# Cumulative sums of logs as two float32r numbers, and closings of rows moved a step, in an attention and mixture-of-experts kernel

## The chip, the cores and the metric

The program runs on one core of one Trainium2 chip. Its time is the device time of one execution in microseconds (us). Times of the kernel before: a median of 416.69 us over 10 runs (415.75 to 418.52). The profile shown is that of one execution of 416.84 us.

Engines are named as in the profile: PE is TensorE (matmuls), PEld its weight loads, DVE VectorE, ACT ScalarE, POOL GpSimd, SP SyncE, which here only issues transfers.

## The reference

Attention comes first: 4 batches, 8 heads, 768 tokens, head size 48. For every batch and head a 48 x 48 state is carried over the tokens, with one decay per key channel:

```python
f = 1.0 / (1.0 + np.exp(-f_logit))
for t in range(S):
    state = f[:, :, t, :, None] * state + np.einsum('bhd,bhe->bhde', k[:, :, t], v[:, :, t])
    y[:, :, t] = np.einsum('bhd,bhde->bhe', q[:, :, t], state)
```

The heads of a token are joined to rows x (3072 x 384). A gate picks one of 4 groups for each row, a second gate one of the group's 4 experts; each gate's weight is that of a softmax. The result of a row is

```python
out[tok_idx] = (g_w * e_w)[:, None] * (np.maximum(x @ w1[g, e], 0.0) @ w2[g, e])   # w1 384 x 1024, w2 1024 x 384
```

## The kernel before

**Units and stages.** The 768 tokens are cut into 6 chunks of 128. A chunk with two of the four batches (s = 0 or 1) is a unit; there are 12, numbered 0 to 11 (NU = 12). With cs the running sum over a chunk's tokens of log(1 + exp(-f_logit)), that is of minus log f, the decay from the start of the chunk is exp(-cs). So a unit needs eq = exp(-cs) for q, kh = exp(cs) for k, masked products of the two for the tokens inside the chunk, and the state for what came before. Each unit goes through stages, each a Python generator that is advanced one piece at a time:

- l (load, L568 to L575): transfers of k, q, f and v, issued on SP's queue. `l` of unit j also issues f of unit j+1. The tiles of f rotate over 3 buffers.
- c (bounded, L581): DVE clamps f at -44 (128 x 768 numbers).
- g (gated): ACT makes exp (L591) and log (L594) in place, `nl`. Then for each of the unit's two batches a float32 matmul with the triangle of ones `tri` sums over tokens (L600, `cs`), and ACT makes eq and kh from it (L601, L602). For s = 0 and s = 1 the last row of eq goes to the tile `ends` by a transfer that POOL issues (L607).
- m (multiplied): DVE multiplies q by eq (L620) and k by kh (L623).
- t (turned): PE transposes both (L634), ACT copies them out (L635, Tq and Tk).
- b (decayed, odd units): PE transposes `ends` (L643, gt), ACT copies it (L644, decays).
- s (scored): PE makes the products `ap` of keys and queries (L659), DVE masks them with `tri` into `am` (L662).
- n (stated): PE makes k v (L676, ds); DVE adds it to the old state (L682, sp) and multiplies by the decays (L683).
- w (weighed): PE makes y from the state (L697) and from `am` (L701); ACT copies it to xT (L704).
- d (done): PE multiplies xT by the gates' weights (L717), ACT copies (L719), PE transposes (L722), DVE reduces to logits (L723, `lgs`).
- x (listed): PE transposes xT to rows (L742); ACT copies them. Rows of units 0 to 7 wait in SBUF and are sent later by SP (`send_kept`, letter o); later units' rows are sent by POOL or ACT.

After the second unit of a chunk, `route` (L178 to L256, letter r, a few pieces a step) picks group and expert on DVE, counts rows per expert with small bf16 matmuls (L203, L205, `rk`), gives each row a place (L211 to L224), and adds to a table of rows by place with bf16 matmuls (L251, `tb`, from `ln` L226 and `val` L233). Between val and the table DVE finishes the weight of each row (L236 to L244: sm, ew, ws, meta), POOL puts the token's number beside it (L245) and sends both to the row in DRAM (L246).

**Chunk 3** (CLOSE = NC - 3) ends with a ranking: after its counts DVE ranks the experts (L271 to L289, `who`), and SP loads the weights of those with most rows (L381). Its places lead to `rows_e` (L318), and after L305 POOL fetches the first rows of two experts (L393, `xg`), which waits for the transfers that write rows and weights of chunks 0 to 3. The expert passes follow: PE transposes xg (L429), multiplies by w1 (L439, `hp`) and w2 (L460, L475, `yo`).

**Order.** Orders are written out by hand and kept as written on PE, DVE, ACT and SP (L85, `manual_schedule`); POOL's order is the framework's. `BEGIN` lists the stages of steps 0 to 2, `EVEN` and `ODD` those of a step i, `ORDERS` the exceptions (NU-3 is step 9, NU-2 step 10, and so on). A token such as `g+1` is the next piece of stage g of unit i+1. A step in the middle takes 10.7 us. In step i PE turns and scores unit i, sums the logs of unit i+1 (after the transposes and before the scores), while c and g prepare the logs of unit i+2. So DVE clamps unit i+2 behind `am`, ACT makes its exp and log behind that. In an odd step b and the update of the state of unit i-1 stand ahead of the sums; in even steps of 4, 6, 8 and 10 tb and the closing of the rows' weights stand after them. PSUM has 8 banks, shared by all products.

Before the loop of steps (L839) SP sends two small "blank" transfers (L841, L842) for row 0 of the rows in DRAM.

## Time and profile before

| | |
|---|---|
| profiled execution | 416.84 us: span 415.0 and 1.84 around it |
| median of 10 runs | 416.69 us |
| attention until the first hp | 137.37 us from the span's start |
| busy: PE, DVE, ACT, POOL | 98%, 64%, 38%, 20% |
| L600 cs, mean of 48 records | 507 ns (a float32 matmul leaves two records) |
| cs of an even step (72.94 us) to the next matmul | 1.29 us |
| am of step 3, step 9, step 10 start | 43.85, 109.30, 120.11 us |

A line of a timeline gives start, duration, engine, line, operation, output and inputs, shapes, and in brackets how long the engine had been idle and what released it. A line of a group gives, after the count, busy time in us, mean ns of one, and idle time before them with its releasers. "L600" is line 600 of the kernel before. In the rows of slices each digit is a tenth of the span's fortieth; PEclk is the granted clock in tenths of full speed, 9 being 90% or more.

### The profile page before, as it was taken

What the parts mean: (1) busy time and instruction counts of PE and PEld (TensorE: products, weight loads), DVE (VectorE), ACT (ScalarE), POOL (GpSimd) and SP (SyncE); (2) the same over time, 40 slices, a digit from 0 to 9 for tenths busy, and PEclk for the clock granted to TensorE, in tenths of its full rate; (3) what the DMA queues carried; (4) which work ended last, traced back from release to release, by engine and by line L of the source; (5) the groups of instructions that cost most, each with busy time, mean ns of one, the idle gap of its engine ahead of it and who ended that gap; (6) DMA issues with size and microseconds to landing.
All of it is one profiled execution on the core that took longest, in us unless ns stands there. A gap on an engine that the chain in (4) does not pass through costs nothing.

```text
span 415.0 us, 10066 instructions
## 1 busy us (share of the span) xinstructions
PE 405.7 (98%) x4047; PEld 374.7 (90%) x4047; DVE 266.9 (64%) x778; ACT 157.1 (38%) x353; POOL 83.2 (20%) x127
## 2 busy tenths in 40 slices
PE   8999999999998999999999999999999999999995
PEld 3888988888777978989999999999999999999992
DVE  5666887878898731640799767485595595594230
ACT  6777766666555311211223122222231231231220
POOL 4000010101012147001041221311321320120230
PEclk9999999999999999999999999999999999999999
DMA  9999997877999649985729467586595695585010
GB/s 173 213 199 213 187 177 149 152 140 154 285 331 392 201 168 339 390 285 185 276 82 336 134 246 263 163 321 187 189 349 153 235 337 186 204 319 162 28 47 24
DMA packets 132145, 88.98 MB, mean 214 GB/s; under 512 B 102582, under 2 KB 122748, under 8 KB 132090
## 3 DMA queue, kind: packets, MB, share of 16 engines
q1 hardware_dynamic: 125666, 75.50, 62.2%
q0 software_dynamic: 5792, 11.92, 9.6%
q10 hardware_dynamic: 632, 0.83, 0.6%
q8 instruction: 34, 0.56, 0.6%
q14 instruction: 21, 0.17, 0.1%
HBM read 78.71 MB, written 9.83 MB: 213 GB/s over the span
## 4 chain that ended last, share of the span: by engine, by line
PE 48%; issue 30%; DMA 9%; POOL 6%; DVE 4%; ACT 1%; POOLq 1%
PE hp L439 12%; PE yo L475 7%; DMA out_dram<-yt,xg 6%; PE ap L659 5%; PE y L701 5%; PE yo L460 4%; POOL out_dram L450 4%; PE cs L600 4%; POOL xg L393 2%; PE x_ps L742 2%; PE ds L676 2%; PE tr_k L634 2%; PE tr_q L634 2%; PE y L697 2%; DMA xg<-x_dram,rows_e 2%
## 5 line engine op out<-in xcount | busy, mean ns | idle before, releaser
L439 PE MATMUL hp<-xe,w 128*128 128x128 f32 (+14 forms) x864 | 138.6, 320 | 0.0
L439 PEld LDWEIGHTS hp<-xe,w 128*128 128x128 f32 x864 | 135.8, 190 | 0.8
L475 PE MATMUL yo<-h,w 128*128 128x230 f32 (+13 forms) x672 | 115.8, 333 | 0.0
L422 DVE STREAM_TRANSPOSE yr<-yT 32x192 f32<-32x192 f32 (+1 forms) x208 | 70.5, 339 | 70.4 <-ACT yT L476 67.8
L475 PEld LDWEIGHTS yo<-h,w 128*128 128x128 f32 x672 | 113.7, 190 | 0.2
L415 DVE STREAM_TRANSPOSE xe<-xg 32x192 f32<-32x192 f32 (+1 forms) x208 | 69.7, 335 | 8.6 <-PE hp L439 5.6
L440 ACT ACTIVATE h<-hp 128x256 f32<-128x256 f32 (+14 forms) x72 | 34.4, 478 | 103.6 <-PE hp L439 103.6
L450 POOL DMA_INDIRECT out_dram<-yt,xg x32 | 34.4, 1075 | 150.0 <-ACT yt L447 144.4
L476 ACT COPY yT<-yo 128x230 f32<-128x230 f32 (+13 forms) x42 | 13.4, 325 | 80.5 <-PE yo L475 80.5
L393 POOL DMA_INDIRECT xg<-x_dram,rows_p x30 | 29.6, 987 | 51.9 <-DMA out_dram<-yt,xg 28.2
L662 DVE TENSOR_TENSOR am<-ap,tri 128x512 f32<-128x512 f32 x48 | 29.8, 681 | 11.2 <-PE ap L659 11.2
L701 PE MATMUL y<-am,v 128*64 128x128 f32 x384 | 24.7, 276 | 0.6 <-issue 0.4
L701 PEld LDWEIGHTS y<-am,v 128*64 128x64 f32 x384 | 21.1, 137 | 4.0 <-issue 2.5
L659 PE MATMUL ap<-Tq,Tk 48*64 48x128 f32 x768 | 23.8, 273 | 0.0
L659 PEld LDWEIGHTS ap<-Tq,Tk 48*64 48x64 f32 x768 | 20.8, 133 | 1.6 <-issue 1.1
L460 PE MATMUL yo<-w,h 128*128 128x384 f32 x64 | 21.3, 486 | 0.0
L600 PE MATMUL cs<-ld_f,tri 128*128 128x384 f32 x48 | 18.6, 507 | 0.1
L460 PEld LDWEIGHTS yo<-w,h 128*128 128x128 f32 x64 | 11.9, 190 | 7.4
L607 POOL DMA_DIRECT2D ends<-eq x10 | 5.4, 541 | 55.5 <-ACT eq L601 55.5
L447 ACT ACTIVATE yt<-yr,xg 128x384 f32<-128x384 f32 (+13 forms) x26 | 14.4, 604 | 5.4 <-DVE yr L422 5.4
L704 ACT COPY xT<-y 128x512 f32<-128x512 f32 x24 | 13.5, 581 | 5.2 <-PE y L701 5.1
L634 PE MATMUL tr_q<-ident,qh 128*128 128x128 f32 x96 | 14.5, 273 | 0.5 <-issue 0.4
(173 smaller groups left out, 369.4 us busy)
## 6 DMA issues: line engine op xcount, KB each, us to landing
w<-in_moe_w_dram SPq DMA_DIRECT2D x34, 1536.0 KB, 10.5
qh<-in_q_dram SPq DMA_DIRECT2D x12, 384.0 KB, 4.9
ld_k<-in_k_dram SPq DMA_DIRECT2D x12, 384.0 KB, 6.0
v<-in_v_dram SPq DMA_DIRECT2D x12, 384.0 KB, 5.8
ld_f<-in_f_logit_dram SPq DMA_DIRECT2D x11, 384.0 KB, 6.0
x_dram<-x_kept SPq DMA_DIRECT2D x2, 1536.0 KB, 11.1
x_dram<-x POOLq DMA_DIRECT2D x2, 384.0 KB, 7.5
x_dram<-x ACTq DMA_DIRECT2D x2, 384.0 KB, 8.4
```

The lines of the kernel that those rows point to most:

```text
L393: nc.gpsimd.indirect_dma_start(out=w["x"][:, j, :], out_offset=None, in_=x_dram[0:1 + top, :], in_offset=bass.IndirectOffsetOnAxis(ap=rows ...
L415: squares(w, lambda n, k_, rk, g, rg: nc.vector.transpose(out=xT[rg, 0:n, k_], in_=x[rk, 0:n, g]))
L422: squares(w, lambda n, k_, rk, g, rg: nc.vector.transpose(out=y[rk, 0:n, g], in_=yT[rg, 0:n, k_]))
L439: nc.tensor.matmul(hp[:, o, :], lhsT=w1[:, ko, (f + o) * P:(f + o + 1) * P], rhs=w["xT"][:, ko, :], start=(ko == 0), stop=(ko == KO - 1))
L440: nc.scalar.activation(h[:, f:f + 2, :], hp, AF.Relu)
L450: sent = nc.gpsimd.indirect_dma_start(out=out, out_offset=bass.IndirectOffsetOnAxis(ap=w["x"][0:m, j, DM + 1:RW].bitcast(U32), axis=0), in ...
L460: nc.tensor.matmul(yp, lhsT=w["h"][:, fo, :], rhs=w2[:, fo, :], start=(fo == 0), stop=(fo == FO - 1))
L475: nc.tensor.matmul(yp, lhsT=w2[:, fo, m * P:(m + 1) * P], rhs=w["h"][:, fo, :], start=(fo == 0), stop=(fo == FO - 1))
L600: nc.tensor.matmul(cs.rearrange("t h d -> t (h d)"), lhsT=tri, rhs=nl[:, b], start=True, stop=True)
L634: nc.tensor.transpose(out=pt[:, a, :], in_=w[nm + "h"][:, b, 2 * a:2 * a + 2, :].rearrange("t r d -> t (r d)"), identity=ident)
L659: nc.tensor.matmul(ap[r][half, a, :], lhsT=w["Tk"][rows, b, a, half], rhs=w["Tq"][rows, b, a, :], start=True, stop=True)
L701: nc.tensor.matmul(ys[b][DP * h:DP * h + DP, a, :], lhsT=w["v"][:, b, 2 * a + (b ^ h), :], rhs=w["am"][b][:, b ^ h, a, :], start=(c == 0 a ...
```

## The change

- From unit 6 on (SPLIT = 6), the log `nl` is written as two numbers of type float32r: `most`, a copy by ACT, and `least` = nl - most, by POOL. Each sum cs is then two float32r matmuls into the same bank, with `trir`, a float32r copy of `tri`.
- f is loaded a step earlier (f6 behind l4, then always two units ahead), clamped a step earlier (`c+3`, now ahead of the scores of the step, where it stood behind them) and exp, log and `most` come a step earlier (`g+3 g+3`); `least` is made in the step after that (`g+2`). Step 3 (BEGUN) makes both units 5 and 6; step 9 has no clamp and no exp.
- The closing of the rows' weights of chunks 0, 1 and 2 is put off from steps 4, 6 and 8 to a new letter q in steps 5, 7 and 9, ahead of the update of the state. dl and oh get a second buffer for it.
- `val` is made by one operation of twice the width.
- The state is added and multiplied in place, without `sp`.

```diff
--- before.py
+++ after.py
@@ -12,6 +12,7 @@
 I32 = mybir.dt.int32
 U32 = mybir.dt.uint32
 BF16 = mybir.dt.bfloat16
+F32R = mybir.dt.float32r
 AF = mybir.ActivationFunctionType
 OP = mybir.AluOpType
 AX = mybir.AxisListType.X
@@ -89,12 +90,14 @@
 
     tri = const([P, P], FP32, "tri")
     ident = const([P, P], FP32, "ident")
+    trir = const([P, P], F32R, "trir")
     strictb = const([P, P], BF16, "strictb")
     onesb = const([P, P], BF16, "onesb")
     halves = const([P, 2], FP32, "halves")
     make_upper_triangular(nc, tri, val=1.0, diag=True)
     make_identity(nc, ident)
     nc.vector.memset(onesb, 1.0)
+    nc.vector.tensor_copy(trir, tri)
     nc.vector.tensor_tensor(strictb, tri, ident, OP.subtract)
 
 
@@ -175,7 +178,7 @@
     def restart():
         nc.vector.tensor_copy(run, base)
 
-    def route(c, lg, sb, tabled=True, tidy=None, counted=None, ranking=None):
+    def route(c, lg, sb, tabled=True, tidy=None, counted=None, ranking=None, late=None):
 
 
         def tmp(shape, name, dtype=FP32, bufs=1):
@@ -185,9 +188,9 @@
         L = lg.rearrange("p n (a e) -> p (n a) e", e=4)
         mx = tmp([P, B * (G + 1)], "mx")
         nc.vector.reduce_max(out=mx, in_=L, axis=AX)
-        dl = tmp(list(SHP), "dl")
+        dl = tmp(list(SHP), "dl", bufs=2)
         nc.vector.tensor_tensor(dl, L, mx.unsqueeze(2).broadcast_to(SHP), OP.subtract)
-        oh = tmp(list(SHP), "oh")
+        oh = tmp(list(SHP), "oh", bufs=2)
         nc.vector.scalar_tensor_tensor(out=oh, in0=dl, scalar=0.0, in1=firsts, op0=OP.is_ge, op1=OP.mult)
         yield
         best = tmp([P, B * (G + 1)], "best")
@@ -229,22 +232,29 @@
             head = tmp(list(BLK), "head")
             nc.vector.tensor_tensor(head, heads_of.rearrange("p e j -> p (e j)").unsqueeze(1).broadcast_to(BLK), atf[:, :, 1:2].broadcast_to(BLK), OP.is_equal)
             val = tmp([P, 2, B, 2 * GE], "val", BF16)
-            for m in range(2):
-                nc.vector.tensor_tensor(val[:, m], head, part[:, c, :, m:m + 1].broadcast_to(BLK), OP.mult)
-            yield
-        sm = tmp([P, B, G + 1], "sm")
-        nc.vector.reduce_sum(out=sm.rearrange("p n a -> p (n a)"), in_=dl, axis=AX)
-        nc.vector.tensor_scalar(sm, sm, 1e-9, None, OP.add)
-        nc.vector.reciprocal(out=sm, in_=sm)
-        ew = tmp([P, B, G], "ew")
-        nc.vector.tensor_tensor(ew, sm[:, :, 1:G + 1], ohv[:, :, 0, :], OP.mult)
-        ws = tmp([P, B], "ws")
-        nc.vector.reduce_sum(out=ws, in_=ew, axis=AX)
-        meta = tmp([P, B, 2], "meta", bufs=2)
-        nc.vector.tensor_tensor(meta[:, :, 0], ws, sm[:, :, 0], OP.mult)
-        nc.gpsimd.tensor_copy(meta[:, :, 1].bitcast(I32), token[:, c, :])
-        nc.gpsimd.dma_start(out=rows_of(c)[:, :, DM:RW], in_=meta)
-        yield
+            nc.vector.tensor_tensor(val, head.unsqueeze(1).broadcast_to((P, 2, B, 2 * GE)), part[:, c].rearrange("p b m -> p m b").unsqueeze(3).broadcast_to((P, 2, B, 2 * GE)), OP.mult)
+            yield
+
+        def weights_of_rows():
+
+            sm = tmp([P, B, G + 1], "sm")
+            nc.vector.reduce_sum(out=sm.rearrange("p n a -> p (n a)"), in_=dl, axis=AX)
+            nc.vector.tensor_scalar(sm, sm, 1e-9, None, OP.add)
+            nc.vector.reciprocal(out=sm, in_=sm)
+            ew = tmp([P, B, G], "ew")
+            nc.vector.tensor_tensor(ew, sm[:, :, 1:G + 1], ohv[:, :, 0, :], OP.mult)
+            ws = tmp([P, B], "ws")
+            nc.vector.reduce_sum(out=ws, in_=ew, axis=AX)
+            meta = tmp([P, B, 2], "meta", bufs=2)
+            nc.vector.tensor_tensor(meta[:, :, 0], ws, sm[:, :, 0], OP.mult)
+            nc.gpsimd.tensor_copy(meta[:, :, 1].bitcast(I32), token[:, c, :])
+            nc.gpsimd.dma_start(out=rows_of(c)[:, :, DM:RW], in_=meta)
+
+        if late is not None:
+            late.append(weights_of_rows)
+        else:
+            weights_of_rows()
+            yield
         if tabled:
             tb = bank([P, 2, GE, 2], "tb")
             for b in range(B):
@@ -548,6 +558,7 @@
 
         CORNERS = [(b, h) for b in range(2) for h in range(2)]
         KEPT = NU - 4
+        SPLIT = 6
         live = {}
         groups, ends = {}, {}
 
@@ -592,12 +603,23 @@
                 if i:
                     yield
                 nc.scalar.activation(nl[:, b], nl[:, b], AF.Ln, bias=1.0, scale=1.0)
+            pieces = [nl]
+            if i >= SPLIT:
+
+                pieces = [sb.tile([P, 2, H * D], F32R, tag=nm, bufs=n, name=nm) for nm, n in (("most", 2), ("least", 1))]
+                if i == SPLIT:
+                    yield
+                nc.scalar.copy(pieces[0], nl)
+                if i > SPLIT:
+                    yield
+                nc.gpsimd.tensor_tensor(pieces[1], nl, pieces[0].bitcast(FP32), OP.subtract)
             eq, qh, kh = pads["eq"][i % 2], w["qh"], pads["kh"][i % 3]
             w.update(eq=eq, kh=kh)
             yield
             for b in range(2):
                 cs = bank([P, H, D], "cs")
-                nc.tensor.matmul(cs.rearrange("t h d -> t (h d)"), lhsT=tri, rhs=nl[:, b], start=True, stop=True)
+                for n, piece in enumerate(pieces):
+                    nc.tensor.matmul(cs.rearrange("t h d -> t (h d)"), lhsT=trir if i >= SPLIT else tri, rhs=piece[:, b], start=(n == 0), stop=(n == len(pieces) - 1))
                 nc.scalar.activation(eq[:, b, :, 0:D], cs, AF.Exp, bias=0.0, scale=-1.0)
                 nc.scalar.activation(kh[:, b, :, 0:D], cs, AF.Exp, bias=0.0, scale=1.0)
                 if b:
@@ -678,9 +700,8 @@
             dst = new[:, :, :, 0:D]
             gv = w["g"].unsqueeze(3).broadcast_to((P, 2, HP, D))
             if c:
-                sp = sb.tile([P, 2, HP, D], FP32, tag="sp", bufs=1, name="sp")
-                nc.vector.tensor_tensor(sp, old[:, :, :, 0:D], ds, OP.add)
-                nc.vector.tensor_tensor(dst, sp, gv, OP.mult)
+                nc.vector.tensor_tensor(dst, old[:, :, :, 0:D], ds, OP.add)
+                nc.vector.tensor_tensor(dst, dst, gv, OP.mult)
             else:
                 nc.vector.tensor_tensor(dst, ds, gv, OP.mult)
             yield
@@ -768,7 +789,7 @@
         def routed(c):
 
             yield from route(c, groups[c], sb, tidy=fix_early if c == CLOSE + 1 else None, counted=load_early if c == CLOSE else None,
-                             ranking=(lambda pool: ranked(GE, pool)) if c == NC - 1 else None)
+                             ranking=(lambda pool: ranked(GE, pool)) if c == NC - 1 else None, late=closings if c < CLOSE else None)
             if c == CLOSE:
                 choose_early(sb)
                 first.append(early())
@@ -780,20 +801,21 @@
             if gens and next(gens[0], True):
                 gens.pop(0)
 
-        first, routes = [], []
+        first, routes, closings = [], [], []
 
 
 
 
         STAGES = {"c": bounded, "g": gated, "m": multiplied, "t": turned, "s": scored, "n": stated, "w": weighed, "d": done, "x": listed, "b": decayed}
         BEGIN = """c0 g0 p g0 g0 m0 m0 m0 m0 l2 t0 t0 t0 t0 h c1 g1 g1 s0 s0 s0 s0 g1 g1 p w0 w0 n0 m1 m1 m1 m1 l3 h x0 x0 x0
-            t1 t1 t1 t1 b1 c2 g2 g2 s1 s1 s1 s1 p d0 g2 g2 n0 n1 w1 w1 m2 m2 l4 n1
+            t1 t1 t1 t1 b1 c2 g2 g2 s1 s1 s1 s1 p d0 g2 g2 n0 n1 w1 w1 m2 m2 l4 f6 n1
             d0 x1 x1 t2 t2 t2 t2 c3 g3 g3 x1 s2 s2 s2 s2 w2 g3 g3 d1 w2 n2 m3 m3 c4 g4 g4""".split()
         BEGUN = 3
-        EVEN = "l+2 d-2 n-1 r r r x-1 x-1 t t t t g+1 g+1 x-1 r s s s s c+2 w d-1 g+2 w g+2 n m+1 m+1".split()
-        ODD = "l+2 d-2 r r x-1 x-1 t t t t b n-1 g+1 g+1 x-1 r s s s s c+2 w d-1 g+2 w g+2 n m+1 m+1 r n".split()
+        EVEN = "l+2 d-2 n-1 r r x-1 x-1 t t t t c+3 g+1 g+1 x-1 r g+2 g+3 g+3 s s s s w d-1 w n m+1 m+1".split()
+        ODD = "l+2 d-2 r r q x-1 x-1 t t t t b n-1 c+3 g+1 g+1 x-1 r g+2 g+3 g+3 s s s s w d-1 w n m+1 m+1 r n".split()
         ORDERS = {
-            NU - 3: "l+2 o d-2 r r x-1 x-1 t t t t b n-1 r g+1 g+1 x-1 r s s s s c+2 w d-1 g+2 w g+2 n m+1 m+1 r n".split(),
+            BEGUN: "l+2 d-2 r r x-1 x-1 t t t t b n-1 c+3 g+1 g+1 x-1 r g+3 g+3 s s s s c+2 w d-1 g+2 w g+2 n m+1 m+1 r n".split(),
+            NU - 3: "l+2 o d-2 r r q x-1 x-1 t t t t b n-1 r g+1 g+1 x-1 r g+2 s s s s w d-1 w n m+1 m+1 r n".split(),
             NU - 2: "d-2 r x-1 x-1 r t t t t r g+1 g+1 x-1 s s s s w d-1 w n m+1 m+1".split(),
             NU - 1: "d-2 r r n-1 x-1 x-1 t t t t r x-1 r s s s s w b d-1 w r r".split(),
             NU: "d-2 r e d-1 x-1 x-1 d-1 x-1 r r r e e r e r r e r r e r e r r e e e e e".split(),
@@ -811,13 +833,21 @@
                 send_kept()
             elif nm == "h":
                 next(turning)
+            elif nm == "q":
+                for close in closings:
+                    close()
+                closings.clear()
             elif 0 <= i < NU:
                 if nm == "l":
 
+                    ahead = i + 1 if i < BEGUN + 2 else i + 2
                     load(i, ("k", "qh"))
-                    if i + 1 < NU:
-                        load(i + 1, ("f",))
+                    if ahead < NU:
+                        load(ahead, ("f",))
                     load(i, ("v",))
+                    return
+                if nm == "f":
+                    load(i, ("f",))
                     return
                 if (nm, i) not in steps_of:
                     steps_of[nm, i] = STAGES[nm](i)
```

## The prediction

> **What bounds the kernel now.** I read the page's busy rows and slices first, then the groups by shape, then timelines of single steps.
>
> ```profile
> PE 405.7 (98%) x4047; PEld 374.7 (90%) x4047; DVE 266.9 (64%) x778; ACT 157.1 (38%) x353; POOL 83.2 (20%) x127
> PEclk9999999999999999999999999999999999999999
> ```
>
> TensorE bounds the program, at full granted clock in every slice. Time taken from its attention steps moves all that follows, unless another engine ends last in that step. That is so in two places. One is VectorE's ranking step (step 9) and the step behind it:
>
> ```profile
> 109.23 0.16 DVE L289 CAST who<-names 1x2 int32<-1x2 f32 x1
> 109.30 2.46 DVE L662 TENSOR_TENSOR am<-ap,tri 128x512 f32<-128x512 f32 x4
> 110.09 2.83 PE L701 MATMUL y<-am,v 128*64 128x128 f32 x32
> 117.38 0.29 PE L251 MATMUL tb<-val,ln 128*128 128x64 bf16 x4 [0.67 <-DVE val L233]
> ```
>
> There 32 y matmuls take 2.83 us, elsewhere 1.97, because VectorE comes late to am; one step on, PE stands 0.67 us for val. The other place is the hand-over to the experts:
>
> ```profile
> 119.21 0.76 POOL L246 DMA_DIRECT2D x_dram<-meta  x1 [2.37 <-DVE number L293]
> 127.75 1.06 POOL L393 DMA_INDIRECT xg<-x_dram,rows_e  x1 [7.78 <-DVE run L305]
> 134.83 0.52 PE L429 MATMUL xg_ps<-ident,xg 128*128 128x128 f32 x3 [0.90 <-DMA xg<-x_dram,rows_e]
> ```
>
> The fetch reads rows that the meta transfer completes. The first expert product follows at 137.37, and PE is solid from there, so a shift of the fetch is a shift of the end.
>
> **The cumulative sums** of six units (6 to 11, counted from 0) change from float32 to float32r with two summands.
>
> ```profile
> L600 PE MATMUL cs<-ld_f,tri 128*128 128x384 f32 x48 | 18.6, 507 | 0.1
> 63.77 0.19 PE L203 MATMUL rk<-ohe,strictb 128*128 128x64 bf16 x1
> L591 ACT ACTIVATE ld_f<-ld_f 128x768 f32<-128x768 f32 x11 | 9.4, 852 | 4.2 <-DVE ld_f L581 4.2
> ```
>
> One float32 matmul shows as two records, so four records make a unit. They end 1.29 us after their start in even steps (72.94, next matmul 74.23): 0.3225 each. The new unit has four float32r matmuls. No row has that type. Bounds per unit: as float32, two records each, 8 x 0.3225 = 2.58, a loss of 1.29; one record each at that pace, 1.29, no gain; as fast as the fastest weight loads (0.109 each, L717), 0.44, a gain of 0.85. The nearest row is bf16: tb's four matmuls of 64 columns free PE in 0.21 (74.23 to 74.44), and the five rk matmuls' 224 columns also in 0.21 (63.77 to 63.98). Two equations give about 0.55 ns a column and 0.0175 a matmul, so 0.2275 for 384 columns. That is stretched from short matmuls; I take 0.17, midway to 0.109: 0.68 a unit, a gain of 0.61. [...]
>
> Where it counts: sums 6 to 9 run in steps 5 to 8, PE-bound. In the even ones tb comes right behind the sums and val is then just late; I take 0.1 off. So 0.61 + 0.51 + 0.61 + 0.51 = 2.24. Sum 10 in step 9 gains nothing by itself (VectorE ends last there). Sum 11 in step 10 only lets PE reach scores sooner.
>
> The ScalarE copy is at most the 0.85 of the row above: a unit then costs ScalarE some 8.2 of 10.7 us (7.55 us busy between 70.2 and 81.0). GpSimd's subtraction has a whole step's slack. I cost both at nothing; cover gone, the copy costs 0.85 a unit. The extra tri copy at the start lies in VectorE's wait for ident.
>
> **The sixth unit's early load** is the one stall I see added.
>
> ```profile
> 37.59 1.48 SPq L575 DMA_DIRECT2D v<-in_v_dram  x1
> 39.17 1.72 SPq L841 DMA_DIRECT2D x_dram<-blank  x1
> DMA to landing us min/median/max: 6.0/6.4/6.9
> 43.85 2.48 DVE L662 TENSOR_TENSOR am<-ap,tri 128x512 f32<-128x512 f32 x4 [0.94 <-PE ap L659]
> 46.06 1.97 PE L701 MATMUL y<-am,v 128*64 128x128 f32 x32
> L581 DVE TENSOR_SCALAR ld_f<-ld_f 128x768 f32<-128x768 f32 x11 | 6.1, 550 | 1.0 <-DMA ld_f<-in_f_logit_dram 1.0
> ```
>
> SP now issues f6 behind step 3's v, where the blank stood: 39.17. By this tile's own landings it is there at 45.2 to 46.1. Its clamp (0.55) now stands on VectorE ahead of am, so am starts at 45.7 to 46.6, not 43.85. In step 9 the y matmuls ended 3.62 after am's start (112.92 less 109.30). So y ends at 49.3 to 50.2, not at 48.03: a loss of 1.3 to 2.2; I take 1.7. Queued behind the clamp are four am, unit 5's clamp, qh and kh; ScalarE holds exp and log of unit 6 behind it, then lgT and xT, whose readers on PE wait for y anyway. Blank writes, k, qh and v of the next unit move one issue (1.6) back on SP; k's 6 us to landing still end long before use. From step 4 each f is asked for a step ahead and its clamp waits for nothing.
>
> **The weights of rows.** Six VectorE operations (73.80 to 75.08, 1.28 us) leave steps 4, 6, 8 and enter 5, 7, 9 ahead of the state update, with POOL's copy and meta's transfer. In 5 and 7 the update gates only the second half's scores: VectorE waited 1.15 us there for decays (63.19), then 1.38 for scores (65.12), so nothing. In step 9, 1.28 minus that 1.15 leaves 0.17 with rounding of the hand-overs, on the ranking's chain. Meta's rows 0 to 2 are read only at 127.75.
>
> **Clamps and val.** The clamp leaves the VectorE chain of steps 9 and 10: 0.47 between am and kh. One val of 256 columns replaces two at 0.245 spacing; the nearest row of that width takes 0.42 (L276): 0.08 gained. The in-place state update costs the same 1.1 us.
>
> **The sum.** Step 3 +1.7, steps 5 to 8 -2.24: -0.5 at step 9. With +0.17 am of step 9 is 0.3 early, and so the weights' loads that "who" starts. Then -0.47 and -0.08 make the meta transfer about 0.8 early. The fetch takes the meta transfer's 0.8 if this alone ends last, and 0.3 if the transfers that share the saturated DMA do. I take 0.6. The profiled execution is 415.0 + 1.84 around the span = 416.84, 0.15 above the median of 416.69: 416.24, so 416.1 on the median. What a measurement can tell here is 0.2%, 0.83 us.
>
> **Rivals.**
> 1. *The stall at step 3 does not reach PE* (f6 lands by 43.5, or its loss is taken back by slack at the hand-over). For it: PE waits 0.90 at 134.83 already, so the front has play. Against: no f row landed under 6.0. It gives -0.6 - 1.7 = -2.3: 414.4.
> 2. *Slower: float32r at the float32 pace or half of it.* With one record at 0.3225 each, the units gain nothing, steps 3 to 9 keep +1.7 + 0.17, and -0.55 follows: +1.3 to +1.9, 418.2. At two records each, four PE-bound units and the later two add 1.29 each: up to 424. It decides once a matmul of 384 columns takes over 0.26 (the four units then gain 0.25 each instead of 0.61, and -0.6 becomes +0.83). For it: no row has the type; against: bf16's pace. This is also the case that the change does not do what it says.
> 3. *VectorE and GpSimd hold each other up.* GpSimd's subtraction starts when a unit's sums end and so lies beside state update, clamp and am. No row has a GpSimd operation of this size. At nothing it costs nothing. From above: am has some 0.6 us of slack before y, and a clamp pushed by a whole 0.95 (the two-input row of 768) loses 0.35 in each of five steps: +1.75, less 0.6, 417.9. It decides from 0.29 a step (five of them take -0.6 to +0.83). [...] In the trace of before GpSimd computes nothing beside VectorE in these steps, so no row decides.
>
> **How the numbers follow.** As worked 0.46 (own range 415.0 to 417.2: 0.20 under -0.83, 0.25 within, 0.01 above); rival 1 0.23, all faster; rival 2 0.13, all slower; rival 3 0.18, of which 0.14 slower and 0.04 within. Together faster 0.43, same 0.29, slower 0.28. The range leaves out rival 1's better half with a fast float32r below 414.2 and the two-record case and doubled contention above 418.4.
>
> **What would show it.** Right: float32r cs matmuls of about 0.17 in groups that free PE in under 0.75; am of step 3 after a wait for ld_f of 1.4 to 2.3, y of step 3 ending near 49.7; the hand-over about 0.6 before 134.83. Wrong: cs groups of 1.3 or more; am of step 3 on time; clamps or state multiplications stretched beyond 0.6 while GpSimd is busy; sums waiting for GpSimd; xg waiting for something else than the rows.

## The result

The changed kernel takes 432.36 us (median of 9 runs, 430.27 to 434.37) against 416.82 (30 runs). The ratio is 1.0369, 95% interval 1.0352 to 1.0387: 15.5 us slower, where 416.1 with a range to 418.4 was forecast. Its profiled execution has a span of 429.4 us. The first expert product starts at 151.59 us instead of 137.37: 14.2 of the 14.4 us by which the span grew arose in the attention part.

The page of the changed kernel: busy time of the engines, the granted clock by slices, the queue of the loads (packets, MB, their time as a share of 16 engines' span), the chain that ended last by engine, and landings of the loads (count, size, us from issue to landing).

```profile
PE 407.9 (95%) x4047; PEld 378.0 (88%) x4047; DVE 273.6 (64%) x773; ACT 162.7 (38%) x359; POOL 95.9 (22%) x133
...
PEclk9999889999989999999999999999999999999998
...
q1 hardware_dynamic: 125666, 75.50, 67.7%
...
PE 35%; issue 30%; DMA 13%; DVE 10%; POOL 6%; SPq 3%; POOLq 1%; ACT 1%; DVEq 0%
...
qh<-in_q_dram SPq DMA_DIRECT2D x12, 384.0 KB, 6.9
...
v<-in_v_dram SPq DMA_DIRECT2D x12, 384.0 KB, 7.5
```

The same four kinds of line on the page of before:

```profile
q1 hardware_dynamic: 125666, 75.50, 62.2%
...
PE 48%; issue 30%; DMA 9%; POOL 6%; DVE 4%; ACT 1%; POOLq 1%
...
qh<-in_q_dram SPq DMA_DIRECT2D x12, 384.0 KB, 4.9
...
v<-in_v_dram SPq DMA_DIRECT2D x12, 384.0 KB, 5.8
```

Three things are new. PE's share of the ending chain is 35% (before 48%), DMA's and VectorE's are larger. The clock, full in every slice before, falls in two stretches. And queue q1 moves the same 125666 packets and 75.50 MB, but they take 67.7% of the queue time instead of 62.2%; q lands after 6.9 us instead of 4.9, v after 7.5 instead of 5.8.

To place the loss I cut the attention part at the first transposition of q in each step. Step lengths in us ("3 at" is the start of step 3, "hp" that of the first expert product; the column to hp is the rest):

| kernel | 3 at | 3 | 4 | 5 | 6 | 7 | 8 | 9 | 10 | to hp | hp |
|---|---|---|---|---|---|---|---|---|---|---|---|
| before | 39.10 | 10.82 | 10.46 | 10.81 | 10.66 | 10.81 | 10.46 | 11.68 | 10.68 | 11.89 | 137.37 |
| changed | 40.83 | 19.48 | 10.46 | 11.62 | 11.54 | 11.29 | 10.18 | 15.68 | 9.25 | 11.26 | 151.59 |

So 1.7 us are lost before step 3, 8.7 in step 3, 1.9 in steps 5 to 8 and 4.0 in step 9; 2.1 come back after it. In step 6 the loss of 0.9 is a gap of PE of 1.04 us before a y matmul, for which the profile names no releaser. It is 1.32 us in a second profile of the changed kernel and absent in the experiments with the tiles moved back or with unit 6's clamp late. Its cause stays open.

Step 3 of the changed kernel, from its timelines of VectorE, TensorE and SP (start, duration, idle time before and its releaser in brackets), and the same stretch in windows of 2 us (busy PE, PEld, DVE, ACT, POOL with counts; then the granted clock, DMA share, GB/s):

```profile
46.84 1.51 SPq L586 DMA_DIRECT2D ld_f<-in_f_logit_dram  x1
53.38 0.56 DVE L592 TENSOR_SCALAR ld_f<-ld_f 128x768 f32<-128x768 f32 x1 [8.05 <-DMA ld_f<-in_f_logit_dram]
53.86 2.47 DVE L684 TENSOR_TENSOR am<-ap,tri 128x512 f32<-128x512 f32 x4
54.60 3.72 PE L722 MATMUL y<-am,v 128*64 128x128 f32 x31 [6.73 <-DVE am L684]
```

```profile
52.00:54.00 2.00, 0.00 (x0) 0.00 (x0) 0.61 (x2) 0.02 (x1) 0.00 (x0) 0.50 1.30 196
54.00:56.00 2.00, 1.40 (x10) 1.09 (x12) 2.00 (x4) 1.82 (x3) 0.00 (x0) 0.50 1.51 174
```

VectorE waits 8.05 us for the load that unit 6's clamp needs, am stands behind the clamp, and PE 6.73 us behind am. The load is not slow in landing alone: it is issued at 46.84, where I had 39.17, as the loads ahead of it on SP's queue were issued later (the v ahead of it at 43.55 instead of 37.59). And when PE goes on, it does so at half the clock, as the windows show: 31 of the y matmuls take 3.72 us; 32 took 2.83 in step 9 of before, where am set their pace as it does here.

Steps 5 and 9 of the changed kernel (TensorE, GpSimd and VectorE), and below them the sums of step 5 and the multiplication of the state of step 9 before:

```profile
72.77 0.44 PE L622 MATMUL cs<-most,trir 128*128 128x384 f32 x1
73.05 0.33 PE L622 MATMUL cs<-least,trir 128*128 128x384 f32 x1
73.22 0.34 PE L622 MATMUL cs<-most,trir 128*128 128x384 f32 x1
73.40 0.33 PE L622 MATMUL cs<-least,trir 128*128 128x384 f32 x1
73.57 0.20 PE L206 MATMUL rk<-ohe,strictb 128*128 128x64 bf16 x1
74.29 2.67 DVE L592 TENSOR_SCALAR ld_f<-ld_f 128x768 f32<-128x768 f32 x1
74.70 1.84 POOL L615 TENSOR_TENSOR least<-ld_f,most 128x768 fp32r<-128x768 f32 x1
...
118.67 2.79 DVE L704 TENSOR_TENSOR st<-st,decays 128x384 f32<-128x384 f32 x1
119.19 1.85 POOL L615 TENSOR_TENSOR least<-ld_f,most 128x768 fp32r<-128x768 f32 x1
125.00 0.43 PE L722 MATMUL y<-am,v 128*64 128x128 f32 x2 [2.12 <-DVE am L684]
```

```profile
62.38 1.56 PE L600 MATMUL cs<-ld_f,tri 128*128 128x384 f32 x4
105.93 0.56 DVE L683 TENSOR_TENSOR st<-sp,decays 128x384 f32<-128x384 f32 x1 [1.15 <-ACT decays L644]
```

The sums are as fast as forecast: four float32r matmuls from 72.77 to the next matmul at 73.57, 0.80 where the same stretch took 1.39 (62.38 to 63.77). But the clamp behind them takes 2.67 us instead of 0.55: it ends at 76.96, 0.42 after the subtraction on GpSimd (74.70 + 1.84 = 76.54). In step 9 the multiplication of the state takes 2.79 instead of 0.56 and ends 0.42 after the subtraction, too. In step 9 nothing covers it: PE stands 0.96 and 2.12 us, and from 126 to 129 us its clock is 0.55, 0.50 and 0.50.

```profile
126.00:127.00 1.00, 1.00 (x14) 0.93 (x12) 1.00 (x3) 0.00 (x0) 0.00 (x0) 0.55 1.05 356
127.00:128.00 1.00, 1.00 (x13) 1.00 (x12) 1.00 (x2) 0.59 (x1) 0.00 (x0) 0.50 1.07 364
```

### The profile page after: what moved, and what is told of

Read it like the earlier page. It is cut to its first block, busy times and chain, and to the rows that moved or that the text cites. A ratio compares the mean times of both kernels' runs of the same rounds, so it can differ in the third digit from the quotient of the medians.

```text
span 429.4 us, 10075 instructions
## 1 busy us (share of the span) xinstructions
PE 407.9 (95%) x4047; PEld 378.0 (88%) x4047; DVE 273.6 (64%) x773; ACT 162.7 (38%) x359; POOL 95.9 (22%) x133
## 3 DMA queue, kind: packets, MB, share of 16 engines
q1 hardware_dynamic: 125666, 75.50, 67.7%
## 4 chain that ended last, share of the span: by engine, by line
PE 35%; issue 30%; DMA 13%; DVE 10%; POOL 6%; SPq 3%; POOLq 1%; ACT 1%; DVEq 0%
PE hp L449 12%; PE yo L485 6%; DMA out_dram<-yt,xg 6%; PE y L722 4%; PE yo L470 4%; POOL out_dram L460 3%; DMA ld_f<-in_f_logit_dram 3%; SPq L586 3%; POOL xg L403 2%; PE ap L681 2%; DMA ld_k<-in_k_dram 2%; DMA qh<-in_q_dram 2%; DVE am L684 1%; PE ds L698 1%; DVE st L704 1%
## 5 line engine op out<-in xcount | busy, mean ns | idle before, releaser
L722 PE MATMUL y<-am,v 128*64 128x128 f32 x384 | 29.0, 296 | 11.9 <-DVE am L684 9.7
L722 PEld LDWEIGHTS y<-am,v 128*64 128x64 f32 x384 | 24.0, 147 | 16.7 <-DVE am L684 13.2
L592 DVE TENSOR_SCALAR ld_f<-ld_f 128x768 f32<-128x768 f32 (+1 forms) x13 | 10.7, 826 | 11.0 <-DMA ld_f<-in_f_logit_dram 10.9
L457 ACT ACTIVATE yt<-yr,xg 128x384 f32<-128x384 f32 (+13 forms) x26 | 14.4, 604 | 5.4 <-DVE yr L432 5.4
L602 ACT ACTIVATE ld_f<-ld_f 128x768 f32<-128x768 f32 (+1 forms) x13 | 10.6, 813 | 15.0 <-DVE ld_f L592 15.0
```

Source lines behind the costliest of these rows:

```text
L457: nc.scalar.activation(y[0:m], yp[0:m], AF.Copy, scale=w["x"][0:m, j, DM:DM + 1])
L722: nc.tensor.matmul(ys[b][DP * h:DP * h + DP, a, :], lhsT=w["v"][:, b, 2 * a + (b ^ h), :], rhs=w["am"][b][:, b ^ h, a, :], start=(c == 0 a ...
```

## The experiments

What I had not looked at was where the tiles lie. Loads are slower from the first microseconds on, long before step 3; the loads themselves are the same. But the change adds tiles, and the addresses behind them move. From the programs' tables of addresses (bytes in a partition):

```
tile                                       before    changed
f (base mod 512)                            416       416
v, eq, qh, kh, padded to 256 bytes a head  163072    171904    (mod 512: 256, 384)
```

By their shapes in the diff, trir adds 512 bytes, two `most` and one `least` 9216, the second buffers of dl and oh 640, and `sp` takes 1536 away: the 8832 of the table. All but the 640 are multiples of 256, so it is the second buffers of dl and oh, the smallest of these, that put the padded tiles 128 past one.

A load writes rows of 48 numbers, 192 bytes, one per head. In the padded tiles a row started on a multiple of 256 before; now it starts 128 past one and crosses the next. That gave theory A (place of the tiles), and the traces theory C (GpSimd shuts VectorE out). The kernel before was timed again with each group of experiments: 422.14, 416.46, 421.32 and 415.84 us on their chips. So ratios are against it on the same chip, and between groups I compare the step table. Its columns to hp and hp scatter by about 1 us between profiles: the kernel before with its tiles moved by 64 bytes, whose times are those of before (below), has 10.94 and 136.34 there instead of 11.89 and 137.37.

**The kernel before, tiles moved by 128 bytes.**

```diff
+        nc.vector.memset(kept([P, 32], "shift"), 0.0)
         pads = {}
```

> The kernel before, with 128 bytes a partition put ahead of the padded tiles of v, eq, qh and kh; nothing else differs. In the changed kernel these tiles begin 128 bytes past a multiple of 256, before they began on one, and all loads of the first 40 us were issued slower there (2.0 us instead of 1.64 for f, landings of qh 6.9 instead of 4.9). Theory A (the place of the tiles slows the loads): landings of qh and v grow by 1 to 2 us here too, the first step of the loop starts about 1.7 us later, 418 to 421 us in all. Theory B (the slower loads come from the changed order or from something else): landings as before, 416.7 us.

Measured: 425.88, ratio 1.0083 (1.0051 to 1.0115), about 3.5 us. Its queue line and landings:

```profile
q1 hardware_dynamic: 125666, 75.50, 69.0%
ld_k<-in_k_dram SPq DMA_DIRECT2D x12, 384.0 KB, 7.3
v<-in_v_dram SPq DMA_DIRECT2D x12, 384.0 KB, 8.2
```

The same packets take 69.0% instead of 62.2%, with no other edit; step 3 starts at 43.25 instead of 39.10. In this profile the clock also stands at 0.50 from 13 to 19 us (mean of 10 to 20 us: 0.66); with a shift of 96 bytes (below) it does not (1.00), and step 3 starts at 41.06. v lands after 8.2 us; k, whose tiles did not change their place against 512, after 7.3 instead of 6.0, which fits its sharing the queue. Theory A holds.

**The changed kernel, tiles moved back.** In this and all further kernels with the tiles moved back lgT has a single buffer, which makes the room.

```diff
+        nc.vector.memset(kept([P, 96], "shift"), 0.0)
         pads = {}
-            lgT = sb.tile([P, P], FP32, tag="lgT", name="lgT")
+            lgT = sb.tile([P, P], FP32, tag="lgT", bufs=1, name="lgT")
```

> The changed kernel with its padded tiles moved by 384 bytes, so that they begin as before on a multiple of 256 (room comes from a single buffer for lgT). Theory A: landings of qh 5, f 6; am of step 3 waits for f6 about 2 us instead of 8; what is lost from step 5 on to GpSimd (about 6 us) stays: 422 to 425 us. Theory B: 431 to 433 us, with the 8 us wait in step 3.

Measured: 426.15, ratio 1.0105 (1.0073 to 1.0137), instead of 1.0369. The queue is at 60.8%, step 3 starts at 38.86 and lasts 12.04. Steps 5, 7 and 9 remain long; step 6 is that of before.

| kernel | 3 at | 3 | 4 | 5 | 6 | 7 | 8 | 9 | 10 | to hp | hp |
|---|---|---|---|---|---|---|---|---|---|---|---|
| realigned | 38.86 | 12.04 | 10.65 | 11.62 | 10.68 | 11.29 | 10.18 | 16.54 | 9.23 | 11.27 | 142.36 |
| and clamp late | 38.97 | 10.81 | 10.87 | 11.55 | 11.09 | 11.30 | 10.67 | 16.44 | 9.24 | 11.49 | 142.43 |
| and plain sums | 39.18 | 12.10 | 10.65 | 10.82 | 10.46 | 10.81 | 10.46 | 12.20 | 10.13 | 11.69 | 138.50 |

**The same, clamp, exp and log behind the scores.**

```diff
-        ODD = "... b n-1 c+3 g+1 g+1 x-1 r g+2 g+3 g+3 s s s s w d-1 w n m+1 m+1 r n"
+        ODD = "... b n-1 g+1 g+1 x-1 r g+2 s s s s c+3 w d-1 g+3 w g+3 n m+1 m+1 r n"
```

and so in EVEN; in step 3 the same for units 5 and 6.

> As the realigned kernel, but the clamp, exp and log stand behind the scores again, as before (of the same unit as in the changed kernel); the subtraction on GpSimd then runs beside am, which has one input in PSUM. Theory C (clamp, or state multiplication, and subtraction shut each other out): no clamp over 0.6 us, the odd steps lose their 2 us on VectorE, and with no wait in step 3 the float32r gain of four steps shows: 413 to 416 us. Rival D (any VectorE work beside the subtraction is slowed): am grows to over 0.8 us each and the time stays over 419 us.

Measured: 425.74, ratio 1.0088 (1.0062 to 1.0115). The forecast of 413 to 416 failed, for three reasons that its timelines show. Step 9, whose order this edit leaves alone, is still 16.44. With the clamp gone, the subtraction (64.52 to 66.35) shuts out the multiplication of the state instead. And in the even step behind it tb is late; by the profile it waits for Tq, which the ScalarE copy now precedes (its first piece starts 1.64 after its transposition, before it was 0.64). But val ends at 75.39, as late as Tq, since VectorE lost the 1.62 us by which 2.18 exceeds 0.56, so the copy's share of the 0.63 stays open:

```profile
64.59 2.18 DVE L705 TENSOR_TENSOR st<-st,decays 128x384 f32<-128x384 f32 x1 [1.07 <-ACT decays L667]
66.70 2.47 DVE L685 TENSOR_TENSOR am<-ap,tri 128x512 f32<-128x512 f32 x4
75.44 0.29 PE L261 MATMUL tb<-val,ln 128*128 128x64 bf16 x4 [0.63 <-ACT Tq L658]
```

Rival D has nothing for it: am keeps its 2.47 us for four. Step 3 lost nothing here (10.81): its 1.2 us in the realigned kernel are the wait of am for f6.

**The realigned kernel without the pieces.**

```diff
-                pieces = [sb.tile([P, 2, H * D], F32R, tag=nm, bufs=n, name=nm) for nm, n in (("most", 2), ("least", 1))]
-                ...
-                nc.gpsimd.tensor_tensor(pieces[1], nl, pieces[0].bitcast(FP32), OP.subtract)
+                yield
```

> As the realigned kernel, but without the pieces: sums stay single float32 matmuls, so neither the ScalarE copy nor the GpSimd subtraction is there; early loads and clamps, q and the rest stay. Theory C: clamps all 0.55 us; what remains is step 3's wait of about 2 us less what steps 9 and 10 gain: 417 to 418.5 us, that is 5 to 7 us under the realigned kernel. Rival E (the early clamps and the moved closings lose by themselves from step 5 on): over 420 us.

Measured: 423.10, ratio 1.002 (1.0005 to 1.0036): 0.8 us over before, as forecast, but only 3 to 4 us under the realigned kernel, not 5 to 7. Steps 5 to 8 are those of before to 0.2 us. What is left is step 3 (+1.28), step 9 (+0.52) and the gain of step 10 (-0.55). So neither early clamps nor moved closings cost steps 5 to 8 anything, and the pieces cost the realigned kernel 3.9 us at hp instead of gaining.

**The realigned kernel, last unit plain.**

```diff
-            if i >= SPLIT:
+            if SPLIT <= i < NU - 1:
...
+            elif i >= SPLIT:
+                yield
...
```

> The realigned kernel, with the last unit's sums (unit 11) left in float32, so that GpSimd has no subtraction in step 9. In the realigned kernel the state multiplication of step 9 took 2.8 us beside that subtraction; step 9 was 4.9 us longer than before, of which about 3 us under a granted clock of 0.5. Theory C (GpSimd's subtraction shuts VectorE out, PE's gaps then drop the clock): state multiplication 0.56, no drop of the clock in step 9, step 9 back to about 12 us: 4 to 5 us under the realigned kernel, 421 to 422 us where that has 426.2. Rival F (step 9 is long because of the closings of the rows or the moved order): still over 425 us.

Measured: 418.93, ratio 1.0061 (1.0044 to 1.0078). The multiplication of the state in step 9 is back at 0.56, step 9 at 12.16 instead of 16.54, and the clock stays full. So the pieces of one unit, whose subtraction of 1.85 us lay in step 9, cost 4.4 us there. At hp 2.9 are left, as step 10 takes 0.9 and step 3 0.5 more than in the realigned kernel. By the ratios the time fell by 0.44%, 1.8 us, where 4 to 5 were forecast.

```profile
109.18 0.56 DVE L707 TENSOR_TENSOR st<-st,decays 128x384 f32<-128x384 f32 x1
PEclk9999999999999999999999999999999999999998
```

**The subtraction on VectorE**, for units 6 to 9 alone.

```diff
-            if i >= SPLIT:
+            if SPLIT <= i < NU - 2:
-                nc.gpsimd.tensor_tensor(pieces[1], nl, pieces[0].bitcast(FP32), OP.subtract)
+                nc.vector.tensor_tensor(pieces[1], nl, pieces[0].bitcast(FP32), OP.subtract)
...
```

> The realigned kernel, with the subtraction on VectorE (about 0.95 us, just ahead of am) instead of GpSimd, and for units 6 to 9 alone, whose sums run in steps bound by PE. Theory C: no VectorE operation beside another takes longer than in the kernel before; step 3 keeps its 1.3 us, steps 5 to 8 give back 0.4 to 0.6 each: first hp at 136 to 137.3 us, time 0.5 to 1.5 us under before of the same chip. Rival G (the extra pass over 768 numbers on ScalarE, or on VectorE, costs PE as much as the sums gain, since tb waits for Tq or am comes late): steps 5 to 8 no shorter than before, time 1 to 2 us over before.

Measured: 417.78, ratio 1.0041 (1.0024 to 1.0058). Nothing on VectorE is stretched (the subtraction takes 0.95), and steps 5 to 8 are 10.53, 10.39, 10.50 and 10.17: 1.15 us shorter together than before, so the float32r gain reaches PE at last. It is spent in step 3 (12.48), step 4 (11.45) and step 9 (12.19), so the time is 1.7 us over before, where 0.5 to 1.5 under it was forecast.

**The same, unit 6's clamp late in step 3.**

```diff
-            BEGUN: "... b n-1 c+3 g+1 g+1 x-1 r g+3 g+3 s s s s c+2 w d-1 g+2 w g+2 n ...
+            BEGUN: "... b n-1 g+1 g+1 x-1 r s s s s c+2 c+3 w d-1 g+2 w g+2 g+3 g+3 n ...
```

> As the kernel with the subtraction on VectorE, but unit 6's clamp, exp and log stand behind the scores of step 3 instead of ahead of them. If step 3's loss is the wait of am for f6, step 3 takes 10.8 us as before instead of 12.1 and the time falls by 1.0 to 1.3 us against its sibling: 1.5 to 2.8 us under before. If something else costs step 3 that time (the second exp and log on ScalarE), no change.

Measured: 417.23, ratio 1.0019 (1.0009 to 1.0029). Step 3 is 10.82, as expected, but of the 1.66 won 1.08 are lost again in step 4 (12.53), so the time stays over before instead of 1.5 to 2.8 us under it. In step 4 VectorE waits for the copy of unit 6 ahead of am:

```profile
55.85 0.96 DVE L616 TENSOR_TENSOR least<-ld_f,most 128x768 fp32r<-128x768 f32 x1 [2.37 <-ACT most L613]
56.73 2.48 DVE L687 TENSOR_TENSOR am<-ap,tri 128x512 f32<-128x512 f32 x4
```

**The changed kernel again**, on the chip of the last three.

> The changed kernel as it is, on the same chip as its realigned siblings and as the kernel before. If the place of the padded tiles accounts for 6 to 9 us of the change's loss, it is 6 to 9 us over the realigned kernel (426.2 where before had 422.1); if the realigned kernel was faster only because of the chip, 0 to 2 us.

Measured: 430.96, ratio 1.0349 (1.0331 to 1.0366). The step table is that of the first profile to 0.4 us. Against 1.0105 for the realigned kernel, the place of the tiles accounts for about 2.4% of the time: some 10 us, a little over the 6 to 9 expected, though in the kernel before it costs only 3.5. (The two ratios were taken on two chips; the single buffer of lgT, which comes with the move, costs nothing that the steps of the kernel with plain sums would show.)

**The changed kernel, f6's clamp late, tiles left where they are.** The edit is the last diff alone.

> The changed kernel, tiles not realigned, with only unit 6's clamp, exp and log put behind the scores of step 3. If the wait of am for f6 is what the slow loads cost PE (8 us), step 3 falls from 19.5 to 11 to 12 us and the time by 6 to 8 us, to 423 to 425 where the changed kernel has 431; a granted clock of 0.66 in that stretch goes with it. If the slow loads hold back other steps as soon as this wait is gone (k, q or v not there), the gain is under 4 us.

Measured: 431.56, ratio 1.0254 (1.0217 to 1.0291): 0.95% or 4 us less than the changed kernel's 1.0349, and 5.4 us at hp, less than expected. Step 4 gives back 2.2 of it (12.68 instead of 10.46). Step 3 falls from 19.77 to 13.80, not to 11 to 12, for the late clamp still stands ahead of qh and kh on VectorE, and qh is what PE needs next:

```profile
52.99 0.56 DVE L592 TENSOR_SCALAR ld_f<-ld_f 128x768 f32<-128x768 f32 x1 [3.71 <-DMA ld_f<-in_f_logit_dram]
54.57 0.63 PE L656 MATMUL tr_q<-ident,qh 128*128 128x128 f32 x4 [2.74 <-DVE qh L642]
...
119.76 0.43 PE L722 MATMUL y<-am,v 128*64 128x128 f32 x2 [2.12 <-DVE am L684]
```

The last line is of step 9: PE stands 2.12 us, with only 0.22 idle ahead of that, and from 121 to 124 us the clock is 0.50 (mean of 120 to 130 us: 0.83). After the 2.74 us it is 0.50 from 56 to 59 (mean of 50 to 60: 0.83).

So part of what the slow loads cost comes from the early clamp: the change asks for one load more by then and puts an instruction that needs it ahead of PE's suppliers.

**GpSimd's subtraction alone.** The kernel with plain sums, with a subtraction (the log from itself) that nobody reads; it only adds work.

```diff
                 yield
+                nc.gpsimd.tensor_tensor(sb.tile([P, 2, H * D], FP32, tag="least", bufs=1, name="least"), nl, nl, OP.subtract)
```

> The realigned kernel with plain float32 sums, with the subtraction alone added on GpSimd (of the log from itself, into a tile that nobody reads); no ScalarE copy, no float32r. Theory C: in odd steps, where GpSimd comes to it behind the transfer of the rows' weights, the clamp or the state multiplication beside it takes 2.2 to 2.8 us instead of 0.55, step 9 is 4 us longer and the time 2 to 4 us over the plain sums alone (which had 0.2% over before). If the loss came from the copy on ScalarE or from float32r, the time is that of the plain sums.

Measured: 425.68, ratio 1.0089 (1.0065 to 1.0113), against 1.002 without it (on another chip): 2.9 us, within the forecast. But GpSimd came to it elsewhere than expected, at the end of am, as it did not have to wait for the sums here. So step 9 was not 4 us longer (12.15), as had been forecast. Beside it now stands qh, or in step 3 a clamp:

```profile
68.00 2.48 DVE L680 TENSOR_TENSOR am<-ap,tri 128x512 f32<-128x512 f32 x4 [0.67 <-PE ap L677]
69.74 1.46 POOL L611 TENSOR_TENSOR least<-ld_f 128x768 f32<-128x768 f32 x1 [1.47 <-issue]
70.40 1.62 DVE L638 TENSOR_TENSOR qh<-qh,eq 128x768 f32<-128x768 f32 x1
```

qh takes 1.62 instead of 0.95 and ends at 72.02, 0.82 after the subtraction (71.20). am, one of whose inputs lies in PSUM, takes its 2.48 although the subtraction runs beside its last 0.74, which speaks against rival D. So the shutting out is shown without ScalarE's copy and without float32r. The price at hp is 1.6 us, 1.2 of it in step 3, where the clamp of unit 5 takes 1.41 and f6 lands later by 0.5.

**Three units and two closings.** On top of the subtraction on VectorE and the late f6: unit 6 plain, chunk 2's closing back in step 8.

```diff
-            if SPLIT <= i < NU - 2:
+            if SPLIT < i < NU - 2:
-   ... late=closings if c < CLOSE else None)
+   ... late=closings if c < CLOSE - 1 else None)
...
+            NU - 4: "l+2 d-2 n-1 r r r x-1 x-1 t t t t c+3 g+1 g+1 x-1 r g+2 g+3 g+3 s s s s w d-1 w n m+1 m+1".split(),
```

> The kernel with the subtraction on VectorE, the late f6 and realigned tiles, with two more parts undone: unit 6 stays float32 (its extra pieces made step 4 two us longer, as VectorE waited 2.4 us for the ScalarE copy ahead of am), and the closing of chunk 2 returns from step 9 to step 8 (step 9 was 0.5 us longer in all kernels with it). Pieces only for units 7, 8 and 9. Theory: step 4 10.5, step 9 11.7, so the first hp at 135.2 to 136 and the time 1.3 to 2.2 us under before. If steps 4 and 9 are long for another reason (exp and log of two units, the early clamp), no gain against the kernel with four units: 0.5 us or more over before.

Measured: 420.48 against 421.32, ratio 0.9979 (0.9956 to 1.0003). Steps 4 and 9 are back at 10.59 and 11.69, so both reasons hold; hp is at 136.20, a little past the expected 136. The time is 0.9 us under before, less than the expected 1.3 to 2.2, and its interval reaches 1: unclear.

**The same, tiles of f and k moved too.**

```diff
         sb = fast.enter_context(tc.tile_pool(name="sb", bufs=2))
+        nc.vector.memset(sb.tile([P, 24], FP32, tag="shift_f", bufs=1, name="shift_f"), 0.0)
-        nc.vector.memset(kept([P, 96], "shift"), 0.0)
+        nc.vector.memset(kept([P, 8], "shift"), 0.0)
```

> As the kernel with three units and two closings, but the tiles of f and k begin on a multiple of 512 bytes instead of 416 past it, and the padded ones stay on a multiple of 256 (of 512 now). A head's row is 192 bytes: from 416 on, six of eight rows cross a multiple of 256 and three of eight one of 512; from 0 on, four and two of eight. If crossings are what slows a load, f and k land sooner (f 6.0 to about 5.6, their share of queue time falls) and the first 30 us shorten by 0.3 to 1 us: 0.3 to 1 us under its sibling. If only the tiles of v and q matter, no change.

Measured: 419.77, ratio 0.9953 (0.9933 to 0.9972): 0.5% under before, with an interval that stays under 1. Over its sibling the gain is not clear: the intervals overlap, and of the 0.93 by which hp is ahead only 0.24 are there by step 3, while 0.66 lie in the column to hp, which scatters by as much.

| kernel | 3 at | 3 | 4 | 5 | 6 | 7 | 8 | 9 | 10 | to hp | hp |
|---|---|---|---|---|---|---|---|---|---|---|---|
| on VectorE, late f6 | 38.89 | 10.82 | 12.53 | 10.54 | 10.67 | 10.49 | 10.18 | 12.19 | 10.14 | 11.39 | 137.84 |
| three units | 38.94 | 10.81 | 10.59 | 10.81 | 10.44 | 10.49 | 10.18 | 11.69 | 10.14 | 12.11 | 136.20 |
| f and k moved | 38.70 | 10.82 | 10.58 | 10.82 | 10.42 | 10.49 | 10.17 | 11.68 | 10.14 | 11.45 | 135.27 |

**Which places are slow.** Three more moves of the kernel before, with no other edit: the padded tiles by 64 bytes (16 numbers) and by 96 (24), and f and k by 96 with the padded ones on a multiple of 512.

> The kernel before, with its padded tiles moved by 64 bytes: heads' rows of 192 bytes then lie at 64 to 256 and 320 to 512 and cross no multiple of 256. If crossings slow the loads: as before, 0 to 0.2% off, queue time of the loads 62% as before. If any start off a multiple of 128 or 256 slows them: 0.6 to 1% over before, as with the shift of 128 bytes.

> The kernel before, with its padded tiles moved by 96 bytes: every row of 192 bytes crosses a multiple of 256, half of them one of 512, as with the shift of 128 bytes. If crossings slow the loads: 0.6 to 1.2% over before, with a queue time of 67 to 70%. If the start's alignment does and 32-byte steps are as bad as 128: the same, but then the shift of 64 bytes is slow too.

> The kernel before, with the tiles of f and k on a multiple of 512 bytes instead of 416 past one (four of eight rows cross a multiple of 256 instead of six), the padded ones on a multiple of 512. If crossings cost in these loads too: queue time under 62%, 0.1 to 0.4% under before. If not: same.

Measured: 64 bytes 1.0006 (0.9993 to 1.0019); 96 bytes 1.0099 (1.0076 to 1.0122); f and k 0.9979 (0.997 to 0.9988). The queue's lines in this order:

```profile
q1 hardware_dynamic: 125666, 75.50, 62.2%
```

```profile
q1 hardware_dynamic: 125666, 75.50, 69.5%
```

```profile
q1 hardware_dynamic: 125666, 75.50, 61.0%
```

A start 64 past a multiple of 256 is as good as one on it (62.2% in both), since 64 to 256 crosses none; 96 is bad (69.5%), as 128 is (69.0%). So in these runs it is the crossing, not a start off a multiple of 128 or 256. The third line says it for f and k too: four of eight rows across instead of six, 61.0% instead of 62.2%, and the kernel before gains 0.2%. Crossings of 256 and of 512 were not told apart, and why a row across one costs more, no run shows.

## Why the prediction was wrong

- **The bound.** That PE bounds the part, and that a shift of the hand-over is a shift of the end, was right: 14.2 us at hp became 14.4 of span. That PE runs "at full granted clock in every slice" was read from the profile of before and silently taken over: after gaps of 6.7 us, and of 0.96 and 2.12, the clock stood at 0.50 for some microseconds. So a stall cost more than its own length here: 31 of the y matmuls behind the 6.7 us took 3.72 us, where 32 took 2.83 in step 9 of before. The shortest gap with it was one of 2.12 us with 0.22 ahead of it (step 9 of the changed kernel with f6's clamp late), while one of 1.32 us (step 6 in the second profile of the changed kernel) left the clock full (1.00 from 90 to 100 us).
- **The cumulative sums.** Right: 0.80 where 1.39 stood, a gain of 0.59 against 0.61; start to start the matmuls take 0.17 to 0.18, the first of a group 0.28. That this arrives as 2.24 us was wrong: with the subtraction on VectorE for three units, steps 7 and 8 gain 0.32 and 0.28. In step 7 closings, clamp and subtraction together bring am late, so y takes 2.22 us instead of 1.97. In even steps tb waits for val: in the kernel with the subtraction on VectorE and the late f6 it starts 1.10 us behind the sums' start in step 6 (74.44 to 75.54) instead of 1.29, so 0.4 is lost there, not the 0.1 that I took off.
- **"GpSimd's subtraction has a whole step's slack. I cost both at nothing."** This is the first step that failed. The subtraction's slack was right and beside the point: what counts is what its 1.85 us do to VectorE. Rival 3 had the mechanism, but its upper end was a clamp pushed by 0.95, a loss of 0.35 a step; a clamp took 2.67 instead of 0.55, and where VectorE ends last, in step 9, 4.4 us followed. The whole length of GpSimd's instruction, which no row of before gives, was the better bound: the clamp took 2.12 us longer beside a subtraction of 1.84. "No row decides" was a reason for the wide end, not for the narrow one.
- **ScalarE's copy** shows no cost where it stands in the changed kernel, though no run takes it out alone; with it, steps 5 to 8 gained 1.15 us once the subtraction was off GpSimd. Later in the step (the late clamp) Tq came late with it, by a share that stayed open, and made for unit 6 in step 4 it held VectorE for 2.37 us. So the slack depends on the place in the step. (Of the working: 7.55 and 0.85 make 8.4, not 8.2.)
- **The early load of unit 6.** The mechanism was right, and with the loads as they were its size nearly: 1.2 to 1.75 us in four realigned kernels that keep it, of a forecast 1.3 to 2.2 (in the fifth, with GpSimd's subtraction alone, a clamp was stretched in the same step: 2.46). What failed is "SP now issues f6 ... where the blank stood: 39.17": it was issued at 46.84 and the loss was 8.7. Landings and issue times of before were carried over to a program whose tiles lie elsewhere. No term of the sum, and no rival, spoke of addresses. This is the largest part of the error, about 10 us with what is lost before step 3. The place of the tiles shows it: with them moved back the load is issued at 38.41, step 3 lasts 12.04 instead of 19.48, and the whole loses 1.05% instead of 3.49%.
- **The weights of rows.** Free in steps 5 and 7, right. In step 9 it cost 0.5, not 0.17; the clamp and val gained 0.55 in step 10, as worked out.
- **Rivals.** Rival 1 (no stall) was the far side of what came. Rival 2 is out by the sums' rows; its "up to 424" leaves out the +1.3 of its own first case, with which it is about 425.7.

Together the changed kernel's 14.2 us at hp: 1.7 before step 3 and 8.7 in it (slow loads, early clamp, clock), 1.9 in steps 5 to 8 (1.0 as in the realigned kernel, where GpSimd stands against VectorE, and 0.9 in step 6 whose cause is open), 4.0 in step 9 (GpSimd against VectorE, clock), less 2.1.

## What to carry to other kernels

Before costing a change, list which tiles move: an added buffer far from a load's tile can shift it, and no line of the diff shows it. Here rows of 192 bytes that newly crossed a multiple of 256 bytes (half of them one of 512) took the queue's share from 62.2% to 69.0%. Work given to an idle GpSimd is not free because GpSimd is idle: ask which VectorE instruction with two inputs in SBUF, or which clamp, stands beside it, and price it with the whole length of GpSimd's instruction (here 1.85 us, beside which a clamp took 2.67 instead of 0.55 and a state multiplication 2.79 instead of 0.56). Put nothing ahead of PE's suppliers on an engine's list that waits for a load with little slack.

## What was unexpected of the hardware

- Rows of 192 bytes across multiples of 256 (which were not told apart from those of 512): queue time 62.2% to 69.0 to 69.5%, 0.8 to 1.0% of this kernel's time by itself, 2.4% in the changed one.
- A GpSimd operation of 128 x 768 takes 1.83 to 2.05 us with two inputs and 1.46 to 1.47 with one tile as both; VectorE's clamp, state multiplication (two inputs in SBUF) or product beside it ends 0.4 to 0.8 us after GpSimd does, but a clamp that starts 0.2 us ahead of it keeps its 0.55 (steps 6 and 8 of the changed kernel, GpSimd then taking 2.05 and 2.04), and am (one input in PSUM) keeps its 2.47 to 2.48 us for four.
- A float32r matmul of 384 columns takes 0.17 to 0.18 us start to start (0.28 for the first of a group), 3.7 times less than a float32 one (two records of 0.3225).
- In the attention part the granted clock fell to 0.50 for some 3 to 7 us after gaps of PE of 2.12, 2.74 and 6.73 us, not after those of 1.04 and 1.32.
